# Three small edits to an attention and feed-forward kernel: the order of two ScalarE reads, one more pair on the o banks, and a hold of 6 in place of 4

## The chip, the core and the metric

The kernel runs on 1 core of a Trainium2 chip. The metric is the device time of one execution in microseconds (us), as the median of several runs. The kernel before takes 1245.48 us (three runs: 1249.6, 1244.66 and 1245.48).

The engines are named as the profile names them: PE is TensorE (its weight loads are a row of their own, PEld), ACT is ScalarE, DVE is VectorE, POOL is GpSimd, and SP is the engine whose queue issues nearly all DMAs. PSUM is the memory that PE writes its results to, in eight banks; ACT and DVE read it, POOL does not. SBUF is the working memory.

## The reference

```python
# q, k, v: (8, 8, 576, 64); w_in: (512, 2048); w_out: (2048, 512); a: 4 numbers, b: 2 numbers
scores = q @ k.T / sqrt(64)                       # block-causal mask, blocks of 64 positions
attn = softmax(scores);  x = attn @ v             # x becomes (4608 tokens, 512)
h = x @ w_in                                      # (4608, 2048)
P = a[0] + a[1]*h + a[2]*h**2 + a[3]*h**3
Q = 1.0 + abs(b[0])*abs(h) + abs(b[1])*h**2
out = (P / (Q + 1e-6)) @ w_out                    # (4608, 512), float32
```

## The kernel before

**Two parts.** The first part runs attention and, between its pieces, the feed-forward block for the first 10 of the 16 blocks of 128 hidden columns ("phase 0"). The second part, after attention, runs what is left of the feed-forward block ("phase 1"). Numbers in float32 are carried as a high and a low half in the fast format of PE, so most products are three matmuls (high times high, high times low, low times high).

**Attention** goes by pairs of heads, 32 pairs (8 batches of 4). For a pair, `prep` transposes q and k into PSUM (tiles `tp`, L438 and L442) and copies them out in halves (ACT L418, DVE L421). `scores` fills PSUM tiles `s` (L513, L530), DVE takes the row maximum (L548), ACT the exponential (L560), POOL divides by the sum (L572). `transp` transposes the result (tiles `t`, L598) and copies it out. `pv` multiplies with v: pairs 0 to 4 in plain float32 (`pv_early`, L621 and L625), later pairs in halves (L648, L664). A pair's output goes to a scratch in DRAM in two halves: `xh` directly, `xl` after a transfer from one half of the partitions to the other (`xt`, L668) and an add on POOL (L671).

**PSUM banks.** Pool `ps_a` gives attention five banks that rotate under one tag. Pool `ps_o` has the two banks `o0` and `o1`, into which phase 0 accumulates its outputs (L299). Pool `ps_h` has one bank, for `h` (L229) and, at other times, for the conversion of weights. The function `bank` decides where the tiles `t` and `tp` go. `prep` of pair p calls it with p - 1:

```python
if p < LEND:                                        # LEND = 4
    pool, tag = ((ps_a, "a"), (ps_o, "o0"), (ps_o, "o1"))[nbank[0] % 3]
else:
    pool, tag = ps_a, "a"
```

**A unit of phase 0** is two blocks of hidden columns for a chunk of 256 tokens; there are 14 chunks of 5 units, 70 units. `first` (L229) makes `h` with 24 matmuls. ACT reads `h` twice: the absolute value `u` (L236) and the first step of the numerator, `s` = a3 h + a2 (L238). It then makes `v` from `u` (L239). POOL multiplies `u` and `v` (L243), DVE continues the numerator with two more reads of `h` (L244, L245). Only then is the one bank of `h` free for the next unit. `recip` takes the reciprocal by a logarithm and an exponential on ACT (L251, L258) and makes the high half `gh` (DVE L260); `split` makes the low half `gl` on POOL (L275); `second` (L299) multiplies with w_out, 12 matmuls. The buffers `u`, `v` and `s` rotate by two. They are shared with the conversion of the weights that phase 1 needs (L164 to L180), which runs beside pairs 8 to 23.

**What sets the order.** Every step of attention asks for a number of half-units of phase 0, so that `U1` half-units have been asked for near the end of attention: `U1 = 14 * 5 * 2 - HOLD`, with HOLD = 4, which is 136 of 140. What has not been asked for follows attention. Phase 1 begins with chunk 7 (`h_7_0` and on), which needs the output of the very last pair. The program is then put in order by a scheduler, engine by engine, before it runs; on the chip each engine keeps that order, and an instruction waits on semaphores for what it needs.

Of the kernel before, what the change touches and what calls it, by code (L numbers as in the profile page):

```python
# [12 lines left out]
AF = mybir.ActivationFunctionType  # L13
# [9 lines left out]
NCH = NT // CT  # L23
NF = DFF // 128
ALAG2 = 1
LEND = 4
RL = 3
C0 = 0
TP = 0
# [4 lines left out]
KQB = 3  # L34
XB = 3
WR, WF = 1, 4
HOLD = 4
ALAG3 = 10
OFFS = (0,3,5)
TLAG = 6  # L40
# [20 lines left out]
def units_of(ph, c):  # L61
    return NFA // NBU[0] if ph == 0 else NFB if c < NSP else NF
# [11 lines left out]
def attn_ffn_kernel(  # L74
# [11 lines left out]
    nc = tc.nc  # L86
# [97 lines left out]
    class Ffn:  # L184
# [34 lines left out]
        def first(self, ph, c, u):  # L219
# [12 lines left out]
            hf = h.rearrange("p j t -> p (j t)")  # L232
            ut = pool.tile([128, 512], F32, name=f"u{tag}", tag="u", bufs=CBUFS if pool is ffn else 2)
            vt = pool.tile([128, 512], F32, name=f"v{tag}", tag="v", bufs=CBUFS if pool is ffn else 2)
            st = pool.tile([128, 512], F32, name=f"s{tag}", tag="s", bufs=CBUFS if pool is ffn else 2)
            nc.scalar.activation(out=ut, in_=hf, func=AF.Abs)  # L236
            if ph == 0:
                nc.scalar.activation(out=st, in_=hf, func=AF.Identity, scale=a3, bias=a2)  # L238
                nc.scalar.activation(out=vt, in_=ut, func=AF.Identity, scale=b1, bias=b0)  # L239
            else:  # L240
                nc.scalar.activation(out=st, in_=hf, func=AF.Identity, scale=na3, bias=na2)  # L241
                nc.gpsimd.tensor_scalar(out=vt, in0=ut, scalar1=b1, scalar2=b0, op0=ALU.mult, op1=ALU.add)  # L242
# [119 lines left out]
    with ExitStack() as actx:  # L362
# [61 lines left out]
        def behind(ins, first):  # L424
            tc.add_manual_dep(ins.ins, first.ins.name,
                              mybir.DependencyInfo(mybir.DependencyClass.NoSync, mybir.DependencyReason.DATA),
                              reason="order")
# [65 lines left out]
        def bank(p, name):  # L493

            if p < LEND:
                nbank[0] += 1
# [240 lines left out]
        there = [((b + 1) * KB + LAST, min(2 * NSP, ((b + 1) * S) // CT)) for b in range(B)]  # L737
        E0, E1, U1 = there[0][0], there[-2][0], there[-2][1] * units_of(0, 0) * 2 - HOLD
        for step in attn_steps():
# [55 lines left out]
```

## Time and profile before

| | |
|---|---|
| median of three runs | 1245.48 us |
| profiled execution, its own time | 1246.05 us |
| its span | 1244.3 us |
| PE busy | 1191.3 us (96%) |
| DVE, ACT, POOL busy | 921.3, 908.5, 876.7 us |
| granted clock of PE, mean | 0.994 |

The span is what the profiler sees, from the first to the last instruction; the execution's own time is 1.75 us longer. A busy PE is not a PE at its peak: a matmul's record includes the time in which it overlaps the next. The table of stages (busy time by stretch of the span) and the chain of waits are of more use here than the shares over the whole span, because attention and the second part have different limits: attention ends at about 821.7 us, the second part is under way from about 841.5 us.

### The profile page before, as it was taken

The page shows a single profiled execution, that of the slowest core. Times are in us where ns is not written, and L with a number is a line of the kernel's source. Part 1 is how long each engine was busy: PE and PEld are TensorE (multiplying, and loading weights), DVE is VectorE, ACT ScalarE, POOL GpSimd, SP SyncE. Part 2 cuts the span into 40 slices and gives each one's busy share as a digit, 9 for nine tenths or more (in the row PEclk, how much of TensorE's full clock was granted, in tenths as well). Part 3 has the DMA queues.
Part 4 walks back from the last instruction along what each step waited for, and adds up shares of the span by engine and source line. Part 5 has one row for each costly group of instructions (what it writes and reads, how often), then busy time and mean ns, then how long its engine had stood idle before and what let it go on. Part 6 is the DMA issues. An engine that isn't in the chain of part 4 may idle for free.

```text
span 1244.3 us, 21931 instructions
## 1 busy us (share of the span) xinstructions
PE 1191.3 (96%) x7124; PEld 1008.8 (81%) x7124; DVE 921.3 (74%) x2016; ACT 908.5 (73%) x2025; POOL 876.7 (70%) x1043
## 2 busy tenths in 40 slices
PE   6888999999999999999999999999999999999998
PEld 4666888888888878888888888878888888888886
DVE  6878888777888777877777777647666766677764
ACT  6877888877988878888888888756555655555554
POOL 4666778877888877787777877756665656665664
PEclk8999999999999999999999999999999999999999
DMA  8782344463544545443333342444014344443100
GB/s 233 208 232 71 94 138 113 121 179 89 143 114 132 132 125 143 108 136 100 100 103 92 105 110 68 113 154 189 1 64 131 120 136 136 136 136 102 43 1 34
DMA packets 199506, 145.67 MB, mean 117 GB/s; under 512 B 136288, under 2 KB 164960, under 8 KB 199392
## 3 DMA queue, kind: packets, MB, share of 16 engines
q1 hardware_dynamic: 196624, 143.15, 40.1%
q10 hardware_dynamic: 2704, 1.11, 0.3%
q8 instruction: 57, 0.93, 0.3%
q14 instruction: 57, 0.47, 0.1%
q0 software_dynamic: 64, 0.00, 0.0%
HBM read 92.28 MB, written 41.94 MB: 108 GB/s over the span
## 4 chain that ended last, share of the span: by engine, by line
PE 71%; ACT 8%; POOL 7%; DVE 5%; DMA 5%; issue 3%; SPq 1%; POOLq 0%; ACTq 0%; DVEq 0%
PE h L229 28%; PE o L299 26%; PE o L664 5%; PE t L598 4%; PE s L530 4%; ACT p L560 2%; PE o L625 2%; POOL gl L275 2%; DMA xt<-xh 1%; POOL u L263 1%; PE tp L438 1%; POOL p L572 1%; PE s L513 1%; DMA wri<-in_moe_w_in_dram 1%; DMA x<-xscr 1%
## 5 line engine op out<-in xcount | busy, mean ns | idle before, releaser
L229 PE MATMUL h<-x,wpi 128*128 128x256 f32 (+1 forms) x2568 | 453.6, 324 | 7.2 <-DMA x<-xscr 2.5
L229 PEld LDWEIGHTS h<-x,wpi 128*128 128x128 f32 x2568 | 380.7, 190 | 53.0 <-issue 6.0
L299 PE MATMUL o<-wpo,gh 128*128 128x512 f32 x1152 | 343.8, 395 | 0.0
L299 PEld LDWEIGHTS o<-wpo,gh 128*128 128x128 f32 x1152 | 212.8, 188 | 43.3 <-issue 0.7
L299 PE MATMUL o<-wpo,gl 128*128 128x512 f32 x576 | 210.3, 400 | 8.6 <-POOL gl L275 8.2
L572 POOL TENSOR_SCALAR p<-p,rc 128x128 f32<-128x128 f32 (+4 forms) x288 | 176.1, 623 | 48.4 <-DVE rc L569 32.9
L243 POOL TENSOR_TENSOR u<-v,u 128x512 f32<-128x512 f32 x144 | 187.5, 1302 | 13.2 <-ACT v L239 5.4
L560 ACT ACTIVATE p<-s,nm 128x288 f32<-128x288 f32 (+4 forms) x320 | 168.3, 534 | 25.2 <-DVE nm L548 19.9
L251 ACT ACTIVATE v<-u,qcb 128x512 f32<-128x512 f32 x144 | 105.1, 730 | 82.0 <-POOL u L243 81.7
L244 DVE TENSOR_TENSOR s<-s,h 128x512 f32<-128x512 f32 x144 | 98.5, 684 | 86.4 <-ACT s L241 65.2
L236 ACT ACTIVATE u<-h 128x512 f32<-128x512 f32 x144 | 86.4, 600 | 102.3 <-PE h L229 96.2
L548 DVE TENSOR_REDUCE nm<-s 128x1 f32<-128x128 f32 (+4 forms) x288 | 129.4, 474 | 7.4 <-PE s L513 4.7
L278 POOL TENSOR_TENSOR gl<-s,gh 128x512 fp32r<-128x512 f32 x74 | 95.8, 1294 | 55.0 <-ACT gh L277 54.9
L598 PE MATMUL t<-ident,p 128*128 128x128 f32 x800 | 122.5, 279 | 8.6 <-POOL p L572 4.1
L299 PEld LDWEIGHTS o<-wpo,gl 128*128 128x128 f32 x576 | 104.7, 189 | 31.1 <-POOL gl L275 12.4
L611 ACT CAST ptrh<-t 128x512 fp32r<-128x512 f32 (+1 forms) x189 | 98.4, 542 | 36.9 <-PE t L598 36.6
L612 DVE TENSOR_TENSOR ptrl<-t,ptrh 128x512 fp32r<-128x512 f32 (+1 forms) x189 | 115.5, 627 | 11.5 <-ACT ptrh L611 10.4
L242 POOL TENSOR_SCALAR v<-u,bab 128x512 f32<-128x512 f32 x74 | 57.2, 774 | 91.0 <-ACT u L236 90.9
L598 PEld LDWEIGHTS t<-ident,p 128*128 128x128 f32 x800 | 91.0, 141 | 27.8 <-POOL p L572 6.8
L263 POOL TENSOR_TENSOR u<-s,u 128x512 f32<-128x512 f32 x70 | 90.3, 1290 | 30.3 <-DVE u L261 16.2
L245 DVE SCALAR_TENSOR_TENSOR s<-s,coef,h 128x512 f32<-128x512 f32 x144 | 106.2, 738 | 2.4
L530 PE MATMUL s<-k,q 64*128 64x512 f32 (+3 forms) x768 | 86.4, 343 | 6.6 <-ACT p L560 2.9
(110 smaller groups left out, 2031.5 us busy)
## 6 DMA issues: line engine op xcount, KB each, us to landing
x<-xscr SPq DMA_DIRECT2D x44, 256.0 KB, 4.0
xscr<-xl SPq DMA_DIRECT2D x32, 288.0 KB, 2.4
out_dram<-os SPq DMA_DIRECT2D x34, 256.0 KB, 3.3
qr<-in_q_dram SPq DMA_DIRECT2D x64, 128.0 KB, 2.8
kr<-in_k_dram SPq DMA_DIRECT2D x62, 128.0 KB, 2.5
xt<-xh SPq DMA_DIRECT2D x54, 144.0 KB, 2.3
xscr<-xh SPq DMA_DIRECT2D x54, 144.0 KB, 2.5
pscr<-os SPq DMA_DIRECT2D x14, 512.0 KB, 2.7
```

Source lines behind the costliest of these rows:

```text
L229: nc.tensor.matmul(h[:, j, :], lhsT=w.win(f, dc, y), rhs=xs[dc][:, hl, :], start=(dc == 0 and i == 0), stop=(dc == 3 and i == 2))
L243: nc.gpsimd.tensor_tensor(out=ut, in0=vt, in1=ut, op=ALU.mult)
L245: nc.vector.scalar_tensor_tensor(out=st, in0=st, scalar=a1, in1=hf, op0=ALU.add if ph == 0 else ALU.subtract, op1=ALU.mult)
L251: nc.scalar.activation(out=vt, in_=ut, func=AF.Ln, bias=qcb)
L263: nc.gpsimd.tensor_tensor(out=ut, in0=st, in1=ut, op=ALU.subtract)
L299: nc.tensor.matmul(self.o[m], lhsT=g[:, j, ms], rhs=w.wout(f, y), start=(u == 0 and j == 0 and i == 0), stop=(u == nu - 1 and j == NBU[ph] ...
L530: mm = nc.tensor.matmul(s["s", t, h], lhsT=q[hs, x, 128 * t:128 * t + 128], rhs=k[hs, y, 0:128 * (t + 1)], start=(n == 0 and t == i), stop ...
L548: nc.vector.reduce_max(out=nm[:, j:j + 1], in_=s[d, j][:, :w] if i == 4 else s["s", i, j], axis=AX.X, negate=True)
L560: nc.scalar.activation(out=dst, in_=s.pop((d, j2))[:, :w] if i == 4 else s.pop(("s", i, j2)), func=AF.Exp, bias=nm[:, n:n + 1], scale=1.0, ...
L572: nc.gpsimd.tensor_scalar(out=x, in0=x, scalar1=rc[:, j2:j2 + 1], scalar2=1.0, op0=ALU.mult, op1=ALU.mult)
L598: nc.tensor.transpose(ps[:, 128 * x:128 * x + 128], src[:, 128 * kb:128 * kb + 128], ident)
L612: nc.vector.tensor_tensor(out=dl, in0=src, in1=dh.bitcast(F32), op=ALU.subtract)
```

## The change

Three edits, all in the first part. `first` issues ACT's two reads of `h` in the other order for phase 0: the numerator's first step `s` before the absolute value `u`. LEND goes from 4 to 5: the tiles of `transp` of pair 4, and those of `prep` of pair 5, may now take the banks `o0` and `o1` too. HOLD goes from 4 to 6, so `U1` is 134.

```diff
-LEND = 4
+LEND = 5
-HOLD = 4
+HOLD = 6
...
-            nc.scalar.activation(out=ut, in_=hf, func=AF.Abs)
+            if ph:
+                nc.scalar.activation(out=ut, in_=hf, func=AF.Abs)
             if ph == 0:
                 nc.scalar.activation(out=st, in_=hf, func=AF.Identity, scale=a3, bias=a2)
+                nc.scalar.activation(out=ut, in_=hf, func=AF.Abs)
                 nc.scalar.activation(out=vt, in_=ut, func=AF.Identity, scale=b1, bias=b0)
```

The changed program has the same instructions. From L237 on its lines are numbered differently: `s` is L239, `u` L240, `v` L241 in phase 0, and every line from L243 of the kernel before on stands two higher (DVE's L244 is L246).

**ACT, a unit of phase 0.** Names in the rows: `s_1_0` is `s` of chunk 1, unit 0; the phase number is left out, and a number at the end is a buffer's. In brackets stand the counters that a row waits for. Before:

```order
L236 ACTIVATE u_1_0_2643<-h_1_0_2618 128x512 [waits PE_49,Pool_49]
L239 ACTIVATE v_1_0_2644<-u_1_0_2643,bab 128x512 [waits DMAHW7_49,Activation_49]
L652 CAST xh_2070<-o_2_2073 128x2x64 [waits DMAHW5_49,DMAHW4_49,DMAHW6_49,DMAHW3_49,PE_49]
L238 ACTIVATE s_1_0_2645<-h_1_0_2618,coef 128x512 [waits Pool_49]
L666 CAST xh_2070<-o_0_2081 128x512 [waits PE_49]
```

Now:

```order
L562 ACTIVATE p_126,sm_1_2256<-s_1_1_2258,nm_1_2255 128x512 [waits DVE_49]
L239 ACTIVATE s_1_0_2645<-h_1_0_2618,coef 128x512 [waits Pool_49]
L562 ACTIVATE p_126,sm_1_2256<-s_1_0_2257,nm_1_2255 128x512 [waits DVE_49]
L240 ACTIVATE u_1_0_2643<-h_1_0_2618 128x512 [waits Activation_49]
L241 ACTIVATE v_1_0_2644<-u_1_0_2643,bab 128x512 [waits DMAHW1_49,Activation_49]
```

Before, the order of the three is u, s, v in 62 units and u, v, s in 8; 29 other rows of ACT stand between the two reads of `h`, over all units. Now it is s, u, v in all 70, with 8 other rows between the reads. DVE's first read of `h` (L244, now L246) waits for a count on ACT's semaphore. Before, it is the count that the row of `s` (L238) raises, in all 70 units; now it is the count that the row of `u` (L240) raises, in all 70 units. It is in both programs the later of ACT's two reads.

**PE, pair 3's product with v.** The rows `tp_1`, `tp_2` are the transposes for pair 5, `o_0`, `o_1` the product of pair 3. Before:

```order
L438 MATMUL tp_1_1107<-ident,kr_996 128x128 [waits DMAHW3_49,DMAHW2_49,Activation_49]
L438 MATMUL tp_1_1107<-ident,kr_996 128x128 x3
L442 MATMUL tp_2_1114<-ident,tr_997 128x128 [waits DMAHW6_49,DMAHW5_49,Activation_49]
L621 MATMUL o_0_1136<-pt_948,vz 128x64 [waits DMAHW1_49,DVE_49]
L621 MATMUL o_0_1136<-pt_948,vz 128x64 [waits DMAHW4_49]
L625 MATMUL o_1_1137<-pt_948,vz 128x512 [waits DVE_49]
```

Now:

```order
L440 MATMUL tp_1_1107<-ident,kr_996 128x128 [waits DMAHW3_49,DMAHW2_49,Activation_49]
L440 MATMUL tp_1_1107<-ident,kr_996 128x128 x3
L444 MATMUL tp_2_1114<-ident,tr_997 128x128 [waits DMAHW6_49,DMAHW5_49,DVE_49]
L623 MATMUL o_0_1136<-pt_948,vz 128x64 [waits DMAHW1_49,Activation_49]
L623 MATMUL o_0_1136<-pt_948,vz 128x64 [waits DMAHW4_49]
L627 MATMUL o_1_1137<-pt_948,vz 128x512 [waits Activation_49]
```

The row `o_1` waited for DVE, for its copy of pair 5's k out of a `ps_a` bank. It now waits for ACT: for the exponential that reads the scores (4, 1) out of the bank that `o_1` takes.

**PE, the end of attention.** The first row is the last matmul of attention (pair 31). `h_13_4` is the last unit of phase 0, `h_7_1` belongs to phase 1. Before:

```order
L664 MATMUL o_1_11622<-ptrl,vst 128x64
L299 MATMUL o_13_0_11761<-wpo_4_0_1295,gh_13_2_11754 128x512 x2
L299 MATMUL o_13_1_11762<-wpo_4_0_1295,gh_13_2_11754 128x512 x2
L229 MATMUL h_13_4_11776<-x_13_0_11398,wpi_8_0_1517 128x256 x6
L229 MATMUL h_13_4_11776<-x_13_1_11403,wpi_8_2_1563 128x256 x6
L229 MATMUL h_13_4_11776<-x_13_0_11398,wpi_8_0_1517 128x256 x6
L229 MATMUL h_13_4_11776<-x_13_1_11403,wpi_8_2_1563 128x256 x6
```

Now:

```order
L666 MATMUL o_1_11567<-ptrl,vst 128x64
L301 MATMUL o_12_0_11406<-wpo_8_0_1594,gh_12_4_11585 128x512 x2
L301 MATMUL o_12_1_11407<-wpo_8_0_1594,gh_12_4_11585 128x512 x2
L229 MATMUL h_13_1_11605<-x_13_0_11427,wpi_2_0_1098 128x256 x6
L229 MATMUL h_13_1_11605<-x_13_1_11432,wpi_2_2_1133 128x256 x6
L229 MATMUL h_13_1_11605<-x_13_0_11427,wpi_2_0_1098 128x256 x6
L229 MATMUL h_13_1_11605<-x_13_1_11432,wpi_2_2_1133 128x256 x6
L229 MATMUL h_13_4_11800<-x_13_0_11427,wpi_8_0_1517 128x256 x6
```

Behind attention there stood one `first` (unit 13_4) and three `second`s. Now there stand four `first`s (13_1 to 13_4) and six `second`s. Counted along PE's rows, the units whose `first` is done when a pair's scores begin are: at pair 6, 1.0 before and 1.0 now; at pair 7, 4.0 and 3.0; at pair 12, 17.0 and 14.5; at pair 20, 36.0 and 34.0; at pair 31, 66.0 and 62.8; at attention's end, 69 and 66.

## The prediction

> **What bounds the kernel now.** I read the page's shares first, then the table of stages, then the chain of waits and PE's timeline at the places that the change touches.
>
> The page and the table of stages (start and end in us, length, then busy us and count for PE, PEld, DVE, ACT, POOL, then clock, DMA share and GB/s):
>
> ```profile
> span 1244.3 us, 21931 instructions
> PE 1191.3 (96%) x7124; PEld 1008.8 (81%) x7124; DVE 921.3 (74%) x2016; ACT 908.5 (73%) x2025; POOL 876.7 (70%) x1043
> ```
>
> ```profile
> 62.00:93.00 31.00, 26.83 (x165) 19.31 (x164) 24.24 (x72) 24.13 (x71) 19.36 (x35) 1.00 0.81 229
> 93.00:124.00 31.00, 25.98 (x168) 19.93 (x168) 24.99 (x66) 24.33 (x65) 20.63 (x33) 1.00 0.28 75
> ...
> 900.00:1000.00 100.00, 100.00 (x443) 82.81 (x442) 68.45 (x103) 57.92 (x95) 61.35 (x55) 1.00 0.33 108
> ```
>
> ```profile
> 124.00:310.00 186.00, 177.81 (x1229) 154.96 (x1228) 147.64 (x352) 153.14 (x365) 144.54 (x178) 0.99 0.45 122
> 310.00:600.00 290.00, 279.28 (x1941) 244.08 (x1939) 234.11 (x573) 243.38 (x585) 232.41 (x288) 0.99 0.46 125
> 600.00:780.00 180.00, 179.04 (x1254) 157.98 (x1254) 136.32 (x343) 149.61 (x360) 140.17 (x177) 1.00 0.37 98
> 780.00:845.00 65.00, 60.99 (x373) 51.83 (x372) 39.35 (x82) 43.74 (x94) 41.76 (x47) 1.00 0.48 151
> ```
>
> In the second part PE is busy for the whole of 900 to 1000: nothing that the change does reaches in there. Before it, PE's idle time is what can be won: 9.2 us in 62 to 124 (62 - 26.83 - 25.98), 8.2 us in 124 to 310, 10.7 us in 310 to 600, 1.0 us in 600 to 780 and 4.0 us in 780 to 845. DVE, ACT and POOL are near 80% in the two stages from 124 to 600, so PE is the first limit there but not by much, and an idle gap closed on PE is not always a gap won. The three edits touch three of these places: pair 3 to pair 6 (LEND), the bank of `h` all along (the swap), and the end of attention (HOLD).
>
> **LEND.** PE's timeline at pairs 3 to 6; in brackets PE's idle time before the row, and what ended it. The group of waits under it gives us in all, times, and the longest.
>
> ```profile
> 76.38 0.98 PE L530 MATMUL s<-k,q 64*128 64x512 f32 x6 [0.39 <-ACT p L560]
> ...
> 84.47 5.61 PE L625 MATMUL o<-pt,vz 128*128 128x512 f32 x20 [1.79 <-DVE k L421]
> ...
> 120.69 3.13 PE L229 MATMUL h<-x,wpi 128*128 128x256 f32 x24 [0.77 <-DVE wao L168]
> 126.96 3.10 PE L229 MATMUL h<-x,wpi 128*128 128x256 f32 x24 [1.00 <-DVE s L245]
> ```
>
> ```profile
> PE o L625 <- DVE k L421: 3.0, 2, 1.8
> ```
>
> At 84.47 pair 3's product stands 1.79 us because its `ps_a` bank still holds pair 5's k transposes, which DVE has not copied out. With LEND at 5 these go to `o0` or `o1`; the row now waits for an exponential of pair 4's second group of scores, and those scores are the row at 76.38, 8 us earlier. The wait goes: -1.8 us. The second of the two (1.2 us, pair 4's product behind pair 6's transposes) stays, since `bank` is called with 5 there. Bounds: 0, if the 1.8 us comes back one pair later because DVE and ACT, at 24 to 25 of 31 us each, set the pace; and -3.0 if both go. I take the lower middle, -1.8, since PE is what stands at this row. `o0` and `o1` are still free: the first `second` comes after pair 5's scores begin.
>
> The scheduler has also put other matmuls ahead of the next two rows. `h` of unit 1 (0.77 us, the bank held by a weight conversion) has moved behind pair 6's third group of scores and pair 5's last transposes; unit 2 (1.00 us) has moved behind pair 5's product with v and pair 6's first transposes, some 4 us of PE work where 2 us stood. That is 1.77 us of waits with cover now. I take -1.6; bounds 0 and -1.8.
>
> **The swap.** What it could win is the time for which `h` holds its one bank. The rows: PE's waits for the release, DVE's waits for ACT, and what ACT's read of `h` lasts (min/median/max ns).
>
> ```profile
> PE h L229 <- DVE s L245: 2.2, 4, 1.0
> ...
> DVE s L244 <- ACT s L238: 20.7, 31, 1.7
> ```
>
> ```profile
> L236 ACT ACTIVATE u<-h x144: 577/598/704, 99.3 to 1228.1; 128x512 f32<-128x512 f32 x144
> ```
>
> If DVE could start after `s` alone, `h` would be free 0.6 us earlier in each unit, and the four waits, 2.2 us, would nearly go. But the changed program's DVE row waits for the count that `u` raises, in all 70 units, though it neither reads nor writes `u`. As before, it starts after both of ACT's reads. So where the two reads follow each other directly nothing is won. Something is won in the 8 units where `v` stood between them, and where ACT's head waited for the buffer of `u` while `s` could have run; but none of those stands in the four waits. I take -0.3. Bounds: -2.2, all four waits gone; and +1.0, because `s` now stands at ACT's head when its own buffer is late, with exponentials and copies of attention queued behind it (in the row of unit `s_1_0` it waits for POOL alone).
>
> The Trainium skill, page "PSUM — Partial Sum Buffer", section "PSUM bank collisions raise a hardware error", says that no two engines may access one bank and quadrant at once, two reads included, and that a scheduler therefore orders ScalarE against VectorE there. By that rule the head start can't exist in any order of the two reads; without it the sum below would be lower by about 1.9 us. No run here shows a collision; the row of DVE's waits only agrees with it.
>
> **HOLD.** Three units more follow attention. The chain of waits there (start, length, what), PE's timeline, and the stage:
>
> ```profile
> 822.84 5.02 DMA xt<-xh
> ...
> 828.03 1.44 POOL xl L671
> ...
> 829.48 5.87 DMA xscr<-xl
> ...
> 835.40 2.07 DMA x<-xscr
> ```
>
> ```profile
> 833.23 0.73 PE L299 MATMUL o<-wpo,gl 128*128 128x512 f32 x2 [0.81 <-POOL gl L275]
> 837.61 1.62 PE L229 MATMUL h<-x,wpi 128*128 128x512 f32 x6 [1.36 <-DMA x<-xscr]
> 841.46 0.74 PE L229 MATMUL h<-x,wpi 128*128 128x512 f32 x2 [0.40 <-DVE s L245]
> ```
>
> ```profile
> 821.70:841.50 19.80, 17.22 (x86) 13.78 (x85) 6.69 (x11) 9.07 (x16) 11.33 (x11) 1.00 0.82 259
> ```
>
> Attention's last matmul ends at about 821.7; its output is back as input of phase 1 at 837.5, some 16 us later, and PE is idle 2.6 us of the 19.8 (19.80 - 17.22). What a unit costs when PE is never held up:
>
> ```profile
> 359.79 2.88 PE h L229 x24
> ...
> 370.94 2.75 PE o L299 x12
> ```
>
> That is 2.88 + 2.75 = 5.63 us. Now four `first`s and six `second`s follow attention, 4 x 2.88 + 6 x 2.75 = 28 us against a chain of 16 us. In PE's order 17 us of work stands ahead of the first three matmuls that need pair 31's x. So the 1.36 us goes, and most of the rest; I leave 0.8 us for a `gh` that is due about 8 us after its `h`. That gives -1.8 us; bounds -2.6 and +1. On SP's queue the last `xl` write stood behind three loads of 512 KB for a later chunk; one of the three still does. That can shorten the 5.02 and 5.87 us, which is only margin, since PE's work is longer than the chain.
>
> The three units leave attention, two to two and a half of them before pair 12. In the tail each costs 5.63 us; what does it give back in attention? From 600 to 780 PE has 0.5% idle, so there a unit is worth what it costs. From 124 to 310 PE is idle 4.4%: 2 x 5.63 x 4.4% = 0.5 us is lost at least. The other bound is the pace of the pairs, read from the product with v in the chain:
>
> ```profile
> 49.50 5.61 PE o L625 x20
> ...
> 84.47 5.62 PE o L625 x20
> ...
> 130.42 3.08 PE o L664 x18
> ...
> 299.94 3.24 PE o L664 x20
> ```
>
> Pairs 1 to 3, without units, take (84.47 - 49.50) / 2 = 17.5 us each; pairs 5 to 11 take (299.94 - 130.42) / 6 = 28.3 us, with 16 units over the six pairs from 6 to 12, 2.67 each. So a unit added (28.3 - 17.5) / 2.67 = 4.0 us, an estimate, as the later pairs also have other work. Two units moved then lose 2 x (5.63 - 4.0) = 3.2 us. I take +1.0, nearer the lower bound, because PE is 96% busy there.
>
> **The sum.** -1.8 - 1.6 - 0.3 - 1.8 + 1.0 = -4.5 us. The profiled execution took 1246.05 us (span 1244.3 and 1.75 us around it) and would take 1241.55; the median of the runs is 0.57 us lower, so I forecast 1241.0 us, which is 0.36% less. The terms' bounds add to -10 and +5, but hardly all go one way: 1237 to 1244.5 for this case.
>
> **The rivals.**
>
> *The new order closes more gaps.* PE's 10.7 us of idle time between 310 and 600 belongs to no edit, but every row there has a new place. For it: between the end of one unit's `h` and the start of the next, ten gaps in the old order hold less than 4 us of other PE work and six in the new one (rows counted, each at its usual distance to the next in the trace), against 2.6 us from the end of `h` to its release at the least (two reads by ACT of 0.60 us, and the two rows here). Against it: other waits are not shorter by that, and ACT, at 84% of this stage, leaves little to fill. If half goes, 5.4 us more than forecast: 1235.6 us.
>
> ```profile
> L244 DVE TENSOR_TENSOR s<-s,h 128x512 f32<-128x512 f32 x144 | 98.5, 684 | 86.4 <-ACT s L241 65.2
> L245 DVE SCALAR_TENSOR_TENSOR s<-s,coef,h 128x512 f32<-128x512 f32 x144 | 106.2, 738 | 2.4
> ```
>
> *Nothing is left of it.* The swap does nothing for DVE, as shown, and the gaps at pairs 3 to 6 come back where DVE and ACT set the pace; the tail's gain of 1.8 us pays for the moved units and no more. 1245.5 us.
>
> *The moved units are paid twice.* Slower. If pairs 6 to 12 keep their 28 us although they hold two units fewer, because the softmax chain and the weight conversion on DVE, ACT and POOL set their pace, the two cost their 11.3 us again behind attention: -4.5 - 1.0 + 11.3 = +5.8 us, which makes 1251.3 us. For it: PE idles 4.4% there, and pairs without units need 17.5 us of their own. Against it: a unit cost 4 us in these pairs, not nothing. It decides against the change as soon as the pairs give back less than half of those 11.3 us.
>
> **How the numbers follow.** A run of this kernel tells about 0.5%, 6.2 us, from no change. The forecast case has a chance of 0.40, more gaps closed 0.28, nothing left 0.15, paid twice 0.17. Faster by over 0.5% (below 1239.3) is the second case and a quarter of the first: 0.38. Slower is the last: 0.17. Within 0.5% are the rest, 0.45. The range leaves out a tenth on each side: 1232 to 1250.
>
> **What would show it.** LEND is right if the first L627 row of pair 3 has no wait for DVE k over 0.5 us; HOLD, if PE idles under 1.5 us in the 28 us behind attention, and h L229 no longer waits for x from the scratch there. The swap is as I say if DVE's L246 still begins only after L240 ends, and would be worth more if it begins before. The moved units are right if the pairs 5 to 11 take about 26.5 us each; at 28 the third rival holds. The prediction is wrong above all if PE's idle time between 310 and 600 changes by more than 5 us either way.

## The result, and the profile after

The changed kernel is slower: 1261.21 us (six runs, 1257.71 to 1262.16) against 1247.24 us for the kernel before (six runs on the same chip). The ratio is 1.0111, with a 95% interval of 1.0088 to 1.0133. The forecast was 1241.0 us, the range 1232 to 1250. The profiled execution took 1260.87 us, span 1259.1 us, mean granted clock 0.988 (before 0.994).

The page's shares of the changed kernel, and its table of stages, with the same bounds as before (start and end, length, then busy us and count for PE, PEld, DVE, ACT, POOL, then clock, DMA share, GB/s):

```profile
span 1259.1 us, 21949 instructions
PE 1198.0 (95%) x7124; PEld 1014.6 (81%) x7124; DVE 940.7 (75%) x2016; ACT 911.9 (72%) x2025; POOL 873.9 (69%) x1043
```

```profile
62.00:93.00 31.00, 27.84 (x176) 20.64 (x175) 24.81 (x74) 25.36 (x74) 20.21 (x38) 1.00 0.79 218
93.00:124.00 31.00, 23.65 (x122) 17.39 (x121) 19.16 (x50) 18.16 (x48) 15.27 (x23) 0.83 0.27 78
124.00:310.00 186.00, 175.39 (x1228) 153.08 (x1228) 150.03 (x367) 153.93 (x374) 141.61 (x181) 0.99 0.45 122
310.00:600.00 290.00, 275.74 (x1899) 239.45 (x1896) 238.47 (x566) 240.74 (x579) 229.06 (x287) 0.99 0.45 123
600.00:780.00 180.00, 177.63 (x1248) 156.96 (x1247) 142.53 (x344) 149.81 (x360) 136.61 (x173) 1.00 0.39 101
780.00:845.00 65.00, 61.66 (x401) 54.41 (x401) 44.40 (x80) 47.41 (x95) 47.06 (x50) 0.98 0.54 181
900.00:1000.00 100.00, 100.00 (x443) 82.87 (x442) 67.39 (x98) 57.13 (x93) 59.93 (x54) 1.00 0.30 98
```

The second row stands out: 122 matmuls in 93 to 124 where the kernel before did 168, at a clock of 0.83. The second part is still PE-bound from end to end. What the table can't show is where time is lost for good, since three units have moved out of attention. So I use one measure throughout, on the profiled execution of each kernel: how much later a pair's scores start than in the kernel before, less PE's own time for the difference in phase 0 matmuls done by then (0.120 us for a row of `h`, 0.229 us for a row of `second`, 5.63 us a unit). I call it the **net loss**. For the changed kernel it is +4.6 us at pair 6, +4.4 at pair 13, +12.4 at pair 22, +13.4 at pair 31, and +13.9 at `h_7_4` of phase 1, from where on the two programs run in parallel. So there are two places: pair 5, and pairs 13 to 22.

**Pair 5.** PE's timeline of the changed kernel (in brackets the idle time before the row and what ended it), and then its chain of work that ended last at this place:

```profile
81.39 0.56 PE L623 MATMUL o<-pt,vz 128*128 128x64 f32 x4
81.90 5.61 PE L627 MATMUL o<-pt,vz 128*128 128x512 f32 x20
...
90.37 0.64 PE L515 MATMUL s<-k,qtl 128*128 128x288 f32 x3 [0.98 <-DMA qtl<-qc]
...
94.75 0.60 PE L600 MATMUL t<-ident,p 128*128 128x128 f32 x4
99.80 3.36 PE L229 MATMUL h<-x,wpi 128*128 128x256 f32 x14 [4.45 <-DMA x<-xscr]
103.08 1.86 PE L532 MATMUL s<-k,q 64*128 64x384 f32 x12
...
108.03 7.30 PE L627 MATMUL o<-pt,vz 128*128 128x512 f32 x20 [1.74 <-DVE k L423]
```

```profile
91.67 5.05 DMA xscr<-xl
...
96.76 2.99 DMA x<-xscr
```

The same row of `h` and the same chain in the kernel before:

```profile
97.24 2.05 PE L229 MATMUL h<-x,wpi 128*128 128x256 f32 x15 [0.74 <-DMA x<-xscr]
99.22 1.07 PE L530 MATMUL s<-k,q 64*128 64x384 f32 x12
```

```profile
91.63 2.74 DMA xscr<-xl
94.42 2.78 DMA x<-xscr
```

Pair 3's product with v (the first two rows of the changed kernel) no longer waits, and pair 5 starts 2.7 us earlier (90.37 against 93.07). But in both orders the second half of the first unit's `h` stands ahead of pair 5's third group of scores. It needs pair 3's output, which must first go to the scratch and come back. Before, PE waited 0.74 us for it. Now PE is ready for this row 1.2 us earlier, and x lands 2.6 us later (99.75 against 97.20), so PE stands 4.45 us, with the scores behind it.

That x comes later although pair 3's product ends 2.6 us earlier has two parts. The write of `xl` is issued at the same time as before (91.67 and 91.63), though its data are ready at 88.85 now and were at 91.42 before: SP issues three loads of v, one of `w_out` and the write of `xh` ahead of it, one behind the other from 88.73 on. SP's timeline, the first row of the kernel before, the others of the changed one:

```profile
86.49 0.35 SPq L153 DMA_DIRECT2D wro<-in_moe_w_out_dram  x1
```

```profile
88.73 0.50 SPq L478 DMA_DIRECT2D vz<-in_v_dram  x1
89.33 0.54 SPq L153 DMA_DIRECT2D wro<-in_moe_w_out_dram  x1
...
91.67 0.39 SPq L637 DMA_DIRECT2D xscr<-xl  x1
```

And the write takes 5.05 us in place of 2.74. In all 18 traces the one goes with the other: where a load of `w_out` (512 KB) is issued 1.6 to 1.7 us ahead of the write of `xh`, which goes just ahead of `xl`, the write of `xl` takes 3.3 to 6.0 us; these are the kernels with LEND 5. Where the load stands 3.3 to 5.7 us ahead, with LEND 4, it takes 2.4 to 2.8 us. That the load (tile `wro`) slows the write is a reading of this; no run moves the load alone.

The granted clock in and after that wait:

```profile
94.89:98.30 3.41, 0.46 (x5) 0.22 (x3) 1.99 (x5) 2.59 (x8) 1.52 (x5) 0.99 0.11 17
98.30:105.10 6.80, 5.30 (x27) 4.86 (x28) 0.06 (x1) 0.00 (x0) 1.21 (x2) 0.50 0.27 73
105.10:108.50 3.40, 1.66 (x11) 1.35 (x12) 2.98 (x9) 3.11 (x11) 0.00 (x0) 1.00 0.27 62
108.50:111.90 3.40, 3.40 (x6) 1.66 (x5) 2.97 (x9) 3.37 (x11) 2.65 (x5) 0.50 0.26 54
```

The wait is paid a second time: 6.8 us and then 3.4 us run at half speed, which is why the twenty matmuls of pair 4's product take 7.30 us where pair 3's took 5.61.

**Pairs 13 to 22.** The stretch from the start of pair 13's scores to that of pair 22's, first of the kernel before, then of the changed one:

```profile
308.31:540.12 231.81, 223.49 (x1560) 195.19 (x1559) 189.11 (x465) 194.35 (x470) 185.41 (x233) 0.99 0.48 132
```

```profile
298.32:543.04 244.72, 230.72 (x1588) 199.89 (x1586) 198.38 (x468) 200.09 (x480) 191.51 (x236) 0.99 0.46 124
```

PE is idle 14.0 us in place of 8.3, and the net loss grows by 8.0 us. Half speed has no part in it, 3.4 us in both stretches; the other 2.3 us lie in PE's busy time and are not located. PE's waits in this stretch, in us in all, times and longest, before and after:

```profile
PE t L598 <- DVE ptrl L612: 1.9, 2, 1.3
PE h L229 <- DVE rc L569: 1.6, 1, 1.6
PE o L299 <- POOL gl L275: 1.1, 2, 0.9
```

```profile
PE s L532 <- ACT p L562: 3.3, 4, 1.2
PE o L301 <- POOL gl L277: 2.8, 3, 1.7
PE o L650 <- DVE ptrl L614: 2.2, 2, 1.9
```

No row leads. ACT, POOL and DVE each hold PE up a few times, by one or two us. That is where the prediction had no term at all.

**Over the whole** from 60 us to `h_7_4`, PE is idle 41.5 us in place of 33.7 (+7.8), and runs 23.9 us at half speed in place of 6.8 (8.5 us of full-speed work lost). The sum of the two is somewhat over the 13.9 us; in these two executions about half of the loss is waiting and half is the clock. Over all executions the clock's share is smaller. The profiled execution of the kernel before had a mean clock of 0.994; the 61 others whose clock is on record have a median of 0.991 (0.986 to 0.998), the six of the changed kernel 0.988. By these medians the clock takes about 4 us of the 14 (an estimate: 0.012 of 1259 us less 0.009 of 1245).

**The tail.** The 28 us behind attention's last matmul, first of the kernel before, then of the changed one, with two windows at the end of the second, and PE's timeline there:

```profile
821.71:849.71 28.00, 25.42 (x121) 20.54 (x121) 14.08 (x22) 16.26 (x28) 17.35 (x16) 1.00 0.88 305
```

```profile
816.85:844.85 28.00, 25.23 (x152) 22.12 (x152) 15.72 (x20) 18.88 (x31) 19.82 (x16) 0.96 0.92 326
838.99:842.40 3.41, 1.65 (x6) 0.68 (x5) 3.41 (x5) 2.36 (x4) 3.41 (x3) 0.99 1.03 414
842.40:849.20 6.80, 5.80 (x14) 4.58 (x15) 2.21 (x4) 2.93 (x5) 4.32 (x4) 0.50 1.01 394
```

```profile
840.23 1.21 PE L301 MATMUL o<-wpo,gh 128*128 128x512 f32 x4 [0.81 <-DVE gh L262]
843.40 5.46 PE L229 MATMUL h<-x,wpi 128*128 128x512 f32 x12 [1.96 <-DVE s L247]
```

Nothing waits for x from the scratch any more: that is what HOLD was to do. But PE idles 2.8 us in these 28 us, where it idled 2.6. Two other waits have come, 0.81 us for `gh` and 1.96 us for the bank of `h`, which DVE still reads. They fall close together, and the next 6.8 us run at half speed. From attention's end to `h_7_4` the net loss grows by 1.9 us, from +12.0 to +13.9.

### The profile page after: what moved, and what is told of

It is laid out like the page before. It is cut to its first block, busy times and chain, and to the rows that moved or that the text cites. A ratio compares the mean times of both kernels' runs of the same rounds, so it can differ in the third digit from the quotient of the medians.

```text
span 1259.1 us, 21949 instructions
## 1 busy us (share of the span) xinstructions
PE 1198.0 (95%) x7124; PEld 1014.6 (81%) x7124; DVE 940.7 (75%) x2016; ACT 911.9 (72%) x2025; POOL 873.9 (69%) x1043
## 4 chain that ended last, share of the span: by engine, by line
PE 65%; ACT 10%; DVE 10%; POOL 8%; DMA 3%; issue 3%; SPq 0%; POOLq 0%; ACTq 0%; DVEq 0%
PE h L229 26%; PE o L301 24%; PE o L666 6%; PE s L532 3%; PE t L600 3%; ACT p L562 3%; POOL p L574 2%; POOL gl L277 2%; DVE nm L550 2%; POOL u L265 1%; DVE u L263 1%; DVE gh L262 1%; ACT ptrh L613 1%; DVE ptrl L614 1%; PE o L627 1%
## 5 line engine op out<-in xcount | busy, mean ns | idle before, releaser
L229 PE MATMUL h<-x,wpi 128*128 128x256 f32 (+1 forms) x2568 | 459.8, 326 | 10.1 <-DVE s L247 4.5
L301 PE MATMUL o<-wpo,gh 128*128 128x512 f32 x1152 | 348.3, 395 | 1.8 <-ACT os L311 1.0
L301 PE MATMUL o<-wpo,gl 128*128 128x512 f32 x576 | 215.1, 400 | 5.4 <-POOL gl L277 5.2
L246 DVE TENSOR_TENSOR s<-s,h 128x512 f32<-128x512 f32 x144 | 98.5, 684 | 69.2 <-ACT s L243 46.2
L244 POOL TENSOR_SCALAR v<-u,bab 128x512 f32<-128x512 f32 x74 | 57.0, 771 | 108.6 <-ACT u L237 108.6
L269 DVE SCALAR_TENSOR_TENSOR u<-u,r 128x512 f32<-128x512 f32 x74 | 50.6, 685 | 73.7 <-ACT r L268 72.3
L237 ACT ACTIVATE u<-h 128x512 f32<-128x512 f32 x74 | 44.2, 597 | 79.7 <-PE h L229 79.3
```

Source lines behind the costliest of these rows:

```text
L229: nc.tensor.matmul(h[:, j, :], lhsT=w.win(f, dc, y), rhs=xs[dc][:, hl, :], start=(dc == 0 and i == 0), stop=(dc == 3 and i == 2))
L301: nc.tensor.matmul(self.o[m], lhsT=g[:, j, ms], rhs=w.wout(f, y), start=(u == 0 and j == 0 and i == 0), stop=(u == nu - 1 and j == NBU[ph] ...
```

## The experiments

Three theories stood at the start. *Blocked head*: the first unit's early place at PE, which LEND brings, costs most of the loss. (The place itself is the old one, as the rows above show; what is new is that its x is late.) *Paid twice*: the units moved out of attention save nothing there. *The swap itself*: reading `s` first starts POOL later and costs in every unit. In all 70 units of every kernel here DVE begins only after ACT's second read; so the swap frees `h` no earlier, while, counted from the end of `h` in the changed kernel and the one before, POOL's first multiply starts after 4.83 us (4.34), `gh` comes after 9.60 (9.22) and `gl` after 14.74 (14.48), means over the 70 units. Later a fourth joined them: *the order*, that any new order of the rows loses in the middle pairs.

All results in one table. The ratio is to the kernel before on the same chip. The net loss is given for four stretches of the profiled execution: up to pair 13, pairs 13 to 22, pairs 22 to 31, and from pair 31 to `h_7_4`. The last column is what PE lost to half speed in all, half of the time so spent between 60 us and `h_7_4`. One execution can be read so far only: with HOLD alone, the two numbers that belong to no edit (weights, slow start) and HOLD 16, PE's rows are those of the kernel before up to pair 7 or further, and the net loss at pair 6 is still -0.3, +1.7, +3.2 and +0.5. It differs by how many windows at half speed, 1.7 us each, an execution has ahead of pair 5.

| kernel | median us | ratio (95%) | to 13 | 13-22 | 22-31 | tail | half speed |
|---|---|---|---|---|---|---|---|
| before | 1247.24 | | 0 | 0 | 0 | 0 | 3.4 |
| changed | 1261.21 | 1.0111 (1.0088 to 1.0133) | +4.4 | +8.0 | +1.0 | +0.5 | 11.9 |
| swap alone | 1259.62 | 1.0106 (1.0074 to 1.0137) | +0.7 | +10.2 | +1.9 | -1.5 | 3.4 |
| LEND alone | 1258.45 | 1.0079 (1.0045 to 1.0112) | +7.8 | +6.8 | +2.2 | -0.9 | 10.2 |
| HOLD alone | 1250.3 | 1.0028 (1.0014 to 1.0042) | +0.3 | +2.3 | +1.5 | -0.6 | 10.2 |
| LEND, unit +6 | 1245.18 | 0.9990 (0.9973 to 1.0008) | -4.8 | +2.4 | +1.5 | -1.5 | 3.4 |
| the same again | 1244.88 | 0.9996 (0.9981 to 1.0012) | -4.3 | +2.5 | +1.9 | -1.7 | 5.1 |
| LEND, unit +5 | 1258.34 | 1.0096 (1.0073 to 1.0119) | -1.6 | +12.8 | +1.8 | +2.8 | 11.9 |
| all three, unit +6 | 1261.97 | 1.0117 (1.0088 to 1.0146) | -6.0 | +12.6 | +3.2 | +4.5 | 10.2 |
| no swap | 1255.34 | 1.0078 (1.0046 to 1.0110) | +4.1 | +5.2 | +2.7 | -2.6 | 10.2 |
| weights two steps later | 1261.77 | 1.0115 (1.0087 to 1.0142) | +1.1 | +6.8 | -3.0 | +14.6 | 8.5 |
| slow start longer | 1254.79 | 1.0067 (1.0046 to 1.0088) | +0.6 | +5.9 | +2.9 | -5.0 | 3.4 |
| HOLD 16 | 1273.42 | 1.0215 (1.0186 to 1.0244) | -4.3 | +12.7 | +4.8 | +16.4 | 10.2 |
| changed, seconds far | 1272.2 | 1.0189 (1.0164 to 1.0215) | +10.0 | +11.5 | +0.3 | +6.9 | 11.9 |
| unit +6, seconds far | 1266.18 | 1.0146 (1.0120 to 1.0172) | -1.2 | +13.2 | +1.6 | +8.1 | 11.9 |

### Each edit alone, and LEND with a later first unit

The swap alone is the last hunk of the change's diff; LEND and HOLD alone are one number each. The fourth kernel has LEND 5 and starts phase 0 six steps later, so that the first unit's matmuls stand behind pair 5's third group of scores:

```diff
-LEND = 4
+LEND = 5
...
-            if step >= E0:
+            if step >= E0 + 6:
```

> The swap of ACT's two reads alone; LEND 4 and HOLD 4 as before. Three theories. (A) Blocked head: with LEND 5 the second half of the first unit's h stands on PE ahead of pair 5's third scores, so PE stands 4.45 us for its input and its clock is halved twice: none of that here, 1247 +-3. (B) Paid twice: the units moved behind attention cost 4 to 5.6 us each there and give little back: here 69 units are done at attention's end, as before, so 1247 +-3. (C) The swap itself costs: s at ACT's head holds up what is queued behind it, and POOL's chain starts later: 1251 or more. In all three DVE's first read of h begins only after ACT's second read ends, in all 70 units.

> LEND 5 alone; the swap and HOLD as before. (A) Blocked head: the first unit stands on PE as in the changed kernel, so the wait for x of 4 to 5 us and the half clock between 93 and 112 us come with it: 1254 to 1257, with 1.8 us won at pair 3's product. (B) Paid twice: 69 units at attention's end as before, though one to two fewer around pairs 7 to 15: 1246 to 1249. (C) The swap: nothing of it here, 1246.

> HOLD 6 alone; the swap and LEND as before. The scheduler puts the same 69 units ahead of attention's end as with HOLD 4, so (A), (B) and (C) all say no change, 1247 +-3. If it is slower by 6 us or more, HOLD costs in a way that none of the three names.

> LEND 5 alone, and the first unit is asked for six steps of attention later, so that its h stands behind pair 5's third scores and pair 6's transposes on PE. 69 units at attention's end, as with LEND alone. (A) Blocked head: PE no longer waits for x there, the clock stays whole between 93 and 112 us, and the time falls by 7 to 10 us against LEND alone, to about 1246. (B) Paid twice: the same as LEND alone within 3 us. The edit itself: the first unit is some 10 us later, with 69 units still done, so its own price should be under 2 us.

Alone, the edits cost 12.8, 11.6 and 3.4 us by these medians against their own runs of the kernel before (1246.86 us). That is 28 us for parts whose whole costs 14, so the losses don't add. The later first unit gives back all that LEND lost, 13.3 us. I took that for proof of the blocked head. It was half of one: of the 18.4 us between the two net losses, 12.6 lie ahead of pair 13, where the first unit stands, and 4.4 behind it, in pairs 13 to 22. (That is more than 13.3 because the profiled execution of LEND alone was the slowest of its five, 3.6 us over their median, and the other one 1.5 us under its own.) And in that kernel PE's rows are those of the kernel before again, row for row, from pair 15 on.

### The changed kernel with a later first unit, two numbers that belong to no edit, and HOLD 16

The first takes the three edits and the `E0 + 6` of above. The next two leave the kernel before as it is but for one number each, and the last moves units out of attention without any new order before pair 9:

```diff
-WB0 = 80
+WB0 = 82
```

```diff
-UN = 40
+UN = 44
```

```diff
-HOLD = 4
+HOLD = 16
```

> All three edits, as in the changed kernel, and the condition that starts phase 0 six steps later, so that the first unit's matmuls stand behind pair 5's third scores and pair 6's transposes; 69 units are done at attention's end, as before. Blocked head (the first unit's second half stands at PE's head before its x has arrived, and what this shifts costs the rest): the loss goes, 1244 to 1250 us. The swap costs by itself, through POOL's start on u 0.4 us later in each unit: it stays at 1255 to 1262 us, since the swap is still in. Any new order loses in pairs 13 to 18: between the two, 1250 to 1256 us, with a net loss first seen behind pair 13.

> The kernel before with one number changed that belongs to none of the edits: the conversion of weights starts two steps later (82 in place of 80). The rows are the same up to pair 7, and different from there. If the old order is a narrow optimum and any other order loses in pairs 13 to 18: 1250 to 1260 us. If the loss belongs to the edits: 1244 to 1249 us.

> The kernel before with another such number: the slow start of phase 0 lasts 44 steps in place of 40. The rows are the same up to pair 9 and different from there; 68 units are done at attention's end. Narrow optimum: 1250 to 1260 us. Loss belongs to the edits: 1244 to 1250 us.

> The kernel before with HOLD at 16 alone: the rows are the same up to pair 9, and 67 units are done at attention's end in place of 69, so this prices moved units with the early order kept. Paid back in full (a unit less in attention saves the 5.63 us that it costs behind it): 1244 to 1249 us. Paid twice: 1254 to 1259 us.

The later first unit does in the changed kernel what it did for LEND: at pair 13 the net loss is -6.0 us in place of +4.4, so starting that unit later is worth 10 us there (9 when counted from pair 4, up to which the rows are the old ones). And nothing of it is left at the end: 12.6 us go in pairs 13 to 22 and 4.5 behind pair 31. Two numbers with no bearing on the edits lose 6.8 and 5.9 us in the same pairs. So a loss of that size there needs none of the edits. It does not need every new order either: with HOLD alone PE's rows are new from pair 13 on, and PE idles 8.4 us in these pairs, the kernel before 8.3. Its net loss of 2.3 us there is no more than that of the two kernels with the later first unit (2.4 and 2.5), whose rows are the old ones from pair 15 on.

The kernel with the later weights shows a second loss. All 70 units are done when attention ends in it, and nothing covers the way of the last pair's output through the scratch. Its last stretch, and PE's timeline in it:

```profile
835.43:868.38 32.95, 21.75 (x83) 16.40 (x83) 13.62 (x22) 11.79 (x20) 12.13 (x11) 0.79 0.78 269
```

```profile
840.51 1.65 PE L229 MATMUL h<-x,wpi 128*128 128x512 f32 x6 [1.40 <-DVE xl L667]
845.12 2.02 PE L229 MATMUL h<-x,wpi 128*128 128x512 f32 x6 [2.97 <-DMA x<-xscr]
852.40 2.93 PE L229 MATMUL h<-x,wpi 128*128 128x512 f32 x6 [5.25 <-DMA x<-xscr]
```

11.2 us of 33 idle, and a clock of 0.79: so much can a missing cover cost. HOLD 16 shows the other side. The units are missing inside attention's last pair, whose softmax then stands alone:

```profile
806.00:831.24 25.24, 18.04 (x100) 14.58 (x98) 16.92 (x47) 14.19 (x42) 14.40 (x24) 0.80 0.24 64
```

PE idles 7.2 us of 25, at a clock of 0.80. Of the loss of 16.4 us behind pair 31's start, 10.8 fall in this pair. There, moved units are paid twice. In the changed kernel, which has moved three, the net loss between pair 18 (+12.7) and attention's end (+12.0) doesn't grow: a unit less gives back its 5.63 us.

### The second products further from the first

Pairs 13 to 22 have something in common that looked like a cause: in the trace of the kernel before a unit's `second` starts 12.8 us of PE work behind its `first` (mean), 11.8 to 12.7 in the new orders, while `gl` comes 14.5 us after it. So I ordered each `second` behind the `first` of the unit two further on, in the changed kernel and in the one with the later first unit:

```diff
+                        if ph == 0 and (j, m, i) == (0, 0, 0):
+                            nxt = (0, *divmod(c * nu + u + 2, nu))
+                            if nxt in self.mm:
+                                tc.add_manual_dep(mm.ins, self.mm[nxt].ins.name,
+                                                  mybir.DependencyInfo(mybir.DependencyClass.NoSync, mybir.DependencyReason.DATA),
+                                                  reason="order")
```

(`self.mm` keeps the last matmul of each `first`.)

> The changed kernel, and the second product of each unit of phase 0 ordered behind the first product of the unit two further on (an order of PE's rows alone). Between pairs 13 and 22 a unit's second product now stands 13.6 us of PE work behind its first, 12.1 in the changed kernel and 12.7 in the kernel before (mean over PE's rows); the low half that it needs comes 14.7 us after the first product's end. If seconds that stand too close make the loss between pairs 13 and 22: PE's waits ahead of L301 rows there fall from 9 us to under 4, the net loss of that stretch from 8 us to under 4, and the whole takes 1250 to 1257 us. If the loss there is spread over waits that have nothing in common: the waits come back at other rows, 1258 to 1266 us.

> The changed kernel with the first unit six steps later, and the same order of second products. Beside the run without it (1262 us), if the seconds make the loss: the net loss between pairs 13 and 22 falls from 12.5 us to under 7, 1250 to 1258 us. If not: 1258 to 1266 us.

Both got slower, by 11 and 4 us. In pairs 13 to 22 of the first one PE waits 3.7 us in all ahead of the rows that write `o` tiles (the second products and the products with v), 6.0 in the changed kernel, but 4.0 us ahead of `h` rows in place of 2.1. It idles 14.4 us there in place of 14.0 and spends 13.7 us at half speed in place of 3.4, and the net loss of the stretch is 11.5 us, not 8.0. PE's waits there by name:

```profile
PE h L229 <- DMA x<-xscr: 3.7, 2, 2.1
PE o L302 <- POOL gl L278: 3.2, 3, 1.5
PE s L539 <- ACT p L569: 2.0, 2, 1.1
```

The wait for `gl` is 3.2 us, 2.8 in the changed kernel. The theory fell: moving the second products takes waits from some rows and brings them back at others.

### Without the weight conversion, and the changed kernel without the swap

If nearly every new order loses there, do the pairs lose because the other three engines are full? The conversion of phase 1's weights runs beside pairs 8 to 23. Three kernels leave its arithmetic out, so that phase 1 multiplies with other weights of the same size:

```diff
+                if not there:
+                    for y in range(2):
+                        nc.sync.dma_start(out=self.tile(key)[:, y].bitcast(I32),
+                                          in_=wA.tile((x, f - self.f0, d))[:, y].bitcast(I32))
+                    yield
+                    continue
```

The fourth undoes the swap in the changed kernel.

> The kernel before without the arithmetic of the weight conversion that runs beside pairs 8 to 23: the raw weights are still loaded, and tiles of the first part's weights are written to the scratch in their place, so phase 1 multiplies with wrong weights of the same size. ACT, DVE and POOL lose that work, PE keeps all of its own. It is the yardstick for the next two runs; with less work on three engines 1225 to 1246 us.

> The changed kernel with the same work left out. If the loss between pairs 13 and 22 needs the three engines to be full (any new order is late somewhere, and nothing has room to catch up): net of units it takes the same from pair 13 to pair 22 as the yardstick, within 3 us, and the whole differs by less than 7 us. If the new order itself is worse, whatever the load: 6 us or more in that stretch, and 10 us or more in the whole.

> The changed kernel with the first unit six steps later and the same work left out; with the conversion it lost 12.5 us net between pairs 13 and 22. Full engines: within 3 us of the yardstick there. Order itself: 6 us or more.

> The changed kernel with the swap undone (LEND 5 and HOLD 6 stay); 67 units are done at attention's end. If the swap costs by itself through POOL's later start: 5 us or more under the changed kernel's 1261 us. If any new order loses about the same: 1253 to 1262 us, with a net loss of 4 us or more between pairs 13 and 22.

Medians 1230.57, 1239.16 and 1234.5 us (ratios to the full kernel before 0.987, 0.994 and 0.989, each within 0.003). The stretch from pair 13 to pair 22 in the three, in that order:

```profile
301.53:531.24 229.71, 227.87 (x1613) 201.31 (x1612) 181.57 (x453) 193.31 (x471) 181.32 (x232) 1.00 0.45 120
```

```profile
296.30:542.47 246.17, 244.04 (x1701) 215.00 (x1699) 191.37 (x461) 204.11 (x485) 187.36 (x239) 1.00 0.43 114
```

```profile
302.35:539.88 237.53, 232.25 (x1620) 203.77 (x1618) 186.99 (x455) 197.63 (x477) 176.18 (x232) 0.99 0.44 117
```

PE idles 1.8, 2.1 and 5.3 us there; in the three kernels with the conversion it was 8.3, 14.0 and 16.8 us. The net losses against the first are 2.3 and 6.0 us, with the conversion 8.0 and 12.6. The verdict is split: the first is within the 3 us of "full engines", the second at the 6 us of "the order itself", and the medians' difference of 8.6 us lies between the two bounds. In this stretch more than half of the loss goes with the load, not all; by the medians 14.0 us become 8.6 for the changed kernel, and 16.0 become 3.9 with the later first unit. But the yardstick is not the old order without the load: leaving the arithmetic out gives each of the three kernels new rows, from pair 3 on. So what is shown is that new orders cost PE less waiting where the load is gone, not what the old order would have cost there. It is also shown that work which PE doesn't do costs up to 17.6 us (1248.21 to 1230.57 us, with the new order in it), though the three engines that do it idle for about a fifth of that stretch.

The changed kernel without the swap takes 1255.34 us, 5.9 us less than with it. But the two intervals overlap (1.0046 to 1.0110, and 1.0088 to 1.0133), and its order is another one again. Whether the swap has a price of its own stays open: no experiment could hold the order fixed and swap the reads. The five kernels with the swap lose 8.0 to 13.2 us in pairs 13 to 22, the seven with new rows and without it 2.3 to 12.8.

### One step's difference

The last pair comes closest to holding the edits fixed and changing the order. LEND 5, first unit five steps later in place of six:

```diff
-            if step >= E0 + 6:
+            if step >= E0 + 5:
```

> LEND 5 alone, and the first unit five steps later in place of six: one step's difference from the kernel that took as long as the kernel before. PE's rows of pairs 7 to 11 are those of the kernel before, and from pair 12 on they are new to the end, where with six steps they are the old ones from pair 16 on. If the new order of the middle pairs is what loses: 1250 to 1260 us, with a net loss of 4 to 12 us between pairs 13 and 22. If LEND with a first unit that isn't blocked is as good as the kernel before, whatever the order: 1243 to 1248 us.

> The kernel with LEND 5 and the first unit six steps later once more, in five rounds beside the last: is it faster than the kernel before by what its first pairs gained (2.4 us in its trace)? 1243 to 1246 us, a ratio of 0.997 to 1.000.

1258.34 against 1244.88 us. Both have LEND's transposes in the `o` banks, in neither is the first unit blocked as in the changed kernel (PE waits 1.3 us for its x with five steps, not at all with six; net losses at pair 13 of -1.6 and -4.3 us). With six steps the rows are those of the kernel before from pair 15 on (the expectation says 16), with five they are new from pair 12 on. Pairs 13 to 22, with five and then with six steps:

```profile
305.41:566.17 260.76, 247.04 (x1659) 215.01 (x1658) 208.55 (x479) 208.38 (x497) 200.86 (x243) 0.97 0.44 121
```

```profile
302.72:538.36 235.64, 225.22 (x1572) 196.95 (x1570) 187.33 (x465) 194.68 (x472) 184.55 (x233) 0.99 0.48 130
```

With five steps PE idles 13.7 us (10.4 with six) and spends 17 us at half speed (3.4), and the net loss is 12.8 us (2.5). So at equal edits, but for one step, two orders of the middle pairs differ by some 10 us in these profiles. The profile with five steps is of the slowest of its six executions, 3.6 us over their median, so a part of that may be the execution's; the medians differ by 13.5 us over the whole. The version with six steps is not measurably faster than the kernel before (0.9990 and 0.9996, both intervals hold 1): none beats both.

What makes the old order better than eleven of the twelve others is not settled. The loss isn't one wait, it isn't cured by moving the second products away, and it shrinks with the load of ACT, DVE and POOL. A plain reading, which no run tests, is that the numbers of the kernel before were chosen by its time, so that its order is a lucky one among many, and any edit draws a new one.

## Why the prediction was wrong, step by step

**The step that failed first is a wait that the sum put at nothing: that for x at the first unit's second half, in pair 5.** I priced the wait ahead of pair 3's product (LEND, -1.8) and those ahead of units 1 and 2 (the opening, -1.6). Those three are gone in the changed kernel. But I took for granted that PE, once earlier, would stay so. The trace of before showed the next wait on the way, 0.74 us for x, and I didn't ask whether x would come earlier too. It came 2.6 us later, and the wait became 4.45 us, with 10.2 us at half speed behind it. The forecast for these pairs, LEND and opening together, was -3.4 us; measured +4.6 at pair 6. With the first unit six steps later, four kernels stand at -3.6 to -3.7 there, counted from pair 4, up to which their rows are those of the kernel before. So the terms' size was about right, and their condition was missing.

**The step that failed most is one that the sum didn't have.** A new order for all later rows came in only as an upside (rival *more gaps closed*, 0.28, on a count of gaps behind `h`). Its downside, 8.0 us in pairs 13 to 22, had no price. Of the twelve kernels with new rows there, eleven lost 5.2 to 13.2 us; HOLD alone lost 2.3, no more than the kernels with the old rows. The count of gaps, ten to six, said nothing.

DVE's waits for the row of `u` in the changed kernel (us, times, longest):

```profile
DVE s L246 <- ACT u L240: 13.1, 22, 1.8
```

- *LEND, -1.8:* right at its place. The first L627 row of pair 3 has no wait, and pair 5 starts 2.7 us earlier. The second of the two waits, which was to stay at 1.2 us, is 1.74.
- *The swap, -0.3:* the reason was right: DVE waits for `u` (the row above). I took the Trainium skill, page "PSUM — Partial Sum Buffer", section "PSUM bank collisions raise a hardware error", for it, by which no two engines may access one bank in the same quadrant of partitions at once, two reads included, and the runs agree: in 70 of 70 units of all kernels DVE starts after the second of ACT's reads. I had not priced that POOL's first step starts 0.5 us later, with a bound of +1.0 for other reasons. The swap alone measures +12.8 us, with a new order in it, and nothing separates the two.
- *HOLD, -1.8:* of the two signs named, one was seen, no wait for x. The other was not: PE idles 2.8 us in the 28 us behind attention, and under 1.5 was forecast. The 0.8 us that I left for a `gh` came (0.81); the 1.96 us for the bank of `h`, and 3.4 us lost to half speed right behind it, were not in the term. From attention's end to `h_7_4` it measures +1.9 in place of -1.8.
- *The moved units, +1.0:* of the right size. By the forecast's own measure, from pair 5's product with v to pair 11's, a pair takes 26.5 us ((291.44 - 132.42) / 6), as the sign said, 28.25 before ((299.77 - 130.26) / 6), and from pair 18 on no net loss is added up to attention's end. *Paid twice* is refuted for these three units, and true in HOLD 16, where units go missing in the last pair.
- *What would make it wrong:* I named PE's idle time from 310 to 600 changing by over 5 us. It changed by 3.6 (14.3 against 10.7), so the sign didn't show what it was meant to. Counted by pairs, 13 to 22, it changed by 5.7. The rest of the loss was from 93 to 124 and in the clock, which I had read as 1.00 or 0.99 and left out of every term.
- *The bounds:* the lower ones add to -9.1, not to -10.
- *The side:* slower had 0.17, all of it on a mechanism that was not the one.

## What to carry to other kernels

Where a scheduler writes the order, an edit has two prices: its own, and that of a new order for everything behind it. Here eleven of twelve new orders lost 5 us or more in the middle pairs, more than any term of the sum; a few neutral edits of the kernel before (a start two steps later) measure it before any edit is judged. When a wait is taken out, look up the next one on the same path, and ask when its input arrives, in the DMA queue too. And a window in which PE waits for more than about half of the time costs more than the wait's own length, so a few larger waits can be worse than the same sum in small ones.

## What the runs showed of the chip that I had not expected

PE's granted clock goes to half speed in steps of 3.41 us, and after how busy PE was in the step just before. I laid the clock records of all 18 traces on that grid, from 60 to 1200 us, and counted windows at full speed by PE's busy time:

| PE busy in a window of 3.41 us | windows | next window at half speed |
|---|---|---|
| under 1.5 us | 32 | 32 |
| 1.5 to 1.75 us | 26 | 17 |
| 1.75 to 2.0 us | 52 | 16 |
| 2.0 to 2.25 us | 70 | 2 |
| over 2.25 us | 5729 | 0 |

So PE need not be idle for long. More than 1.9 us of waits in one window always brought a window at half speed, which costs 1.7 us (32 of 32); 1.4 to 1.9 us did so in 33 of 78 windows, and under 1.2 us never did; so waits of the same sum that are spread over two windows can cost nothing more. The changed kernel's rows above show two such windows (0.46 us busy of 3.41 ahead of the half-speed stretch at 98.30, 1.65 ahead of the one at 842.40). The Trainium skill, page "TensorE: Matmul & The Clock Gate", section "What's actually happening", gives the window of 3.4 us and says that an idle window brings the half rate; the traces agree on the window, and put the bound at a window about half busy. Executions of one kernel differ in this: the two profiles of the kernel with six steps lost 3.4 and 5.1 us to it.
